# Batch 1's first dense layer by seven products instead of eight, in a newly planned order (sliding-window attention followed by a squared-ReLU layer, one Trainium2 core)

## The chip, the core and the metric

The kernel runs on one core of one Trainium2 chip. The metric is the device time of one execution in microseconds (us). The kernel before took 212.76 us (median of three runs, 212.1 to 213.73). The profile comes from one execution of its own; its span, from the first to the last instruction, is 210.2 us.

A core has five engines that run at the same time and wait for each other through semaphores: TensorE (PE in the profile, with PEld for its weight loads), VectorE (DVE), ScalarE (ACT), GpSimd (POOL) and SyncE (SP, which here only issues DMAs). TensorE writes to PSUM; VectorE and ScalarE fetch results from there.

## The reference

Four batches of 768 tokens, 8 heads of 64. Each query sees the last 128 keys and the first four ("sinks"). The heads side by side give x with 512 columns, and a dense layer, ReLU, square, dense layer follow:

```python
keep = is_sink | in_window            # 4 sinks, window 128
a = softmax(where(keep, q @ k.T / 8, -1e9))
x = (a @ v)                           # as 3072 tokens x 512
h = x @ w_in                          # 512 x 2048
r = np.maximum(h, 0.0)
g = r * r
return g @ w_out                      # 2048 x 512
```

## The kernel before, in words

A batch is three pairs of token tiles (s = 0, 1, 2, of 256 tokens each). For each pair the attention runs in groups: scores into PSUM (tile `ps`, line 607), the exponential by ScalarE (`expm`, line 628), the mask by VectorE (lines 637, 640) or by a GpSimd select (line 215), the product with the values (`po`, line 676), the normalisation by VectorE (lines 692, 693, into `xn_sb`). Then x is transposed: in batches 0 and 1 by TensorE (`px`, line 725) with a copy into `xT`, in batches 2 and 3 by DMA.

The first dense layer exists in two forms. `layer1` (line 757) is the plain one: 16 blocks of 128 features, four matmuls per block and 256 or 512 tokens; then a ReLU (lines 768, 770) and a square (lines 777, 779) of each PSUM tile. `layer1_fast` is a scheme of the kind of Strassen's: it halves features, inner dimension and tokens, forms sums of the x halves (`xs`, line 845; for one pair of tiles alone they are first spread into `xd`) and of the weights (`weight_sums_in`, `wi`, line 803, and sums written over `w_in_sb`, line 811), and needs seven half-size products instead of eight. The function `quad` makes one group of them: products 1, 2, 5, 4, 3, 6, 7 (line 887) into two PSUM regions, with work between them: a copy `t` of the first region (ScalarE or VectorE, line 189 or 191), two subtractions from it by VectorE (line 928), a ReLU (line 943), and at the end a combined add and ReLU by VectorE alone (line 955), and two squares (lines 909, 911). Product 5 waits for the copy, products 4 and 3 for the two subtractions, 6 and 7 for the ReLU.

Before, batches 2 and 3 use the fast form (pair 0 by itself, in products of 128 columns; pairs 1 and 2 together, in products of 256 columns), batches 0 and 1 the plain one. The second dense layer has the same two forms (`layer2`, line 976, for two thirds of batch 0; `layer2_fast`, line 1086, for all the rest).

All work is recorded as operations in a `Plan` and issued in the order that the string `ORDER` at the top of the file gives: one number for each operation, with a letter where the engine was chosen (d VectorE, a ScalarE, g GpSimd) and a `+n` where a pool of rooms was chosen. PSUM has two pools of two rooms each (`att`, `den`), and an operation may get a room from one or the other. So each engine's queue is fixed by hand ahead of time, in order, and an instruction that waits holds up all behind it on its engine.

`weight_sums_in` keeps two of the five rooms of the pool `qr`, in which the loads of q and k land too. `load_natural` issues the loads of batches 2 and 3 from GpSimd's queue; SyncE transposes q and k by DMA.

Of the kernel before, what the change touches and what calls it, by code (L numbers as in the profile page):

```python
# [21 lines left out]
0 7 8 9 1 5 10 11 2 12 13 3 14 15 55d 57+0 16 19 59a 20 17 56d 21 18 61d 63+0 22 58 62d 65a 60d 64 6 67a 83+1 79 66a  # L22
68d 69+1 85 70 71d 103+0 84+0 105 73g 74d 72d 23 75+1 86 76 77d 91+0 78a 24 87+1 93 25 89 88 92+0 80 26 114+1 90 94
95+0 4 96 117 97 106g 99+1 98 104+0 107 100d 101 118g 81+1 102d 113+0 108d 156 115 127 27 28 29 30 31 32 33 34 35 36
37 38 116d 82 109+0 111 39 40 41 119+1 121 157a 158a 110 112 120 122 162 123+1 125 163d 168 169d 126a 124a 171 172a
170a 159 160d 177 128 131 165 173d 161d 132d 178d 166d 164a 130a 129a 133a 144 146 136 138 174 145 137 289 290 148
134 175a 140 135 176a 147d 167d 139d 291 179d 292 293 141d 142 143 149g 42 43 44 45 46 150 151 47 48 49 50 51 52 53
54 365 366 367 368 208g 369 370 371 372 373 294 295 152 154 296 153d 155d 297d 298d 186 187d 180 181a 200+0 204+1
192+0 201 193 205 194a 206d 195a 189 207d 182d 203a 196+0 197 183 198a 190a 191a 188d 199d 202d 274 212+0+0 184d 209
278 279 215 213 237+0+0 210+1 211 238 240 185d 300 301 275 214 302 241d 276 277 303 280 281 282 304 219+0+0 283 222  # L30
220 306a 305 307 230+0+0 309a 233 231 308 311 223 216 221 310 239d 224+0 312 234g 232g 299 385 386 384 383 313 225
314 242+0 217+0 243 218 284 315 316 235+0 236 285 251+0 286a 287a 317d 252d 253d 244+0 246 226+1 228 247d 227d 245a
248+1 229a 399 322 249d 250d 402 400 323d 355 401 256+0+0 259 257 340 254+0 255 341a 258d 358 356 342a 396 260d 334
335a 374 375 376 377 378 379 380 381 395g 388 390 387 288 392 391 318 389 393 394 331 263+0+0 332a 261+1 264 266 319
262 267d 324d 406 333a 407 320a 337 409 265g 382 597 268+0 598 599 600 601 602 603 604 605 606 607 608 609 610 338a
321d 403 269 328 627d 410 270+0 272 404 408 329a 271a 273d 359 325 405 339a 336a 326a 346 347d 357 327a 415 418 419d
330d 352 411 353a 416 412 354d 447 448 343 344a 345a 349 422 423 425 417g 426g 611 451 452 397 363 449 453d 350d 398
450 351a 348a 454 455 457 466 456a 438 458 459 441 439 467 485 486 489 490 487 460 488 461 361 492 431 491a 432 434
615 413 616 622 620 619 493 462 494d 468 463 464a 414 465 621 617 618 420 440g 612 424g 427 496 433g 442g 428 498
421 470 471 443 435g 436 472a 504a 495 362 499 497 500 473 444 437 508 505 469 628 501 475d 474 477 647 429 625 445  # L40
430 446 650 502a 648 624 503 623 626 360 476 478 481 507 479 506 480 364 482 483d 523+0 525a 524 631 527 526 528 634
632 509+0 510 529 511d 512 530 531a 654 538 633 539 513 514 515 655 533 534 657 649g 656g 516 517a 638 613 614 535
635 536d 537 641 519 520 532a 636 658g 651g 521 639 569+0 570 637 571a 629 583+0 630 572 573 585a 640 522a 518a 574
584 587 575 576 586 555+1 642 589 577a 588 643 679 557a 540 556 590 559 591a 592a 578a 558 560 579 580 593 594 581
561 562 595 541+0 542 683 563a 564a 543d 545 544 680 546 565 547 566 548 684 686 644 567 685a 596a 549a 582a 681
550d 689 682 645 484 646 670 551 552 687 690 673 671 674g 553 688a 554a 663 691 694 666 664 665g 568d 698 692 693
699 659 652 702 703 705 667g 672g 695 696d 700 653 717 660 718 721 668 697 661 736a 704a 669 737 675 676 701 722 739
740 738 708 677 678 662 755+1 706 709 741+1 742 757a 719 720 756 743a 723a 707d 759 745 724 758 761 725 744 760 762
763a 764a 711 746 727 710 713 726a 765 766 747 712 769 714 771 767 728 730 715d 772 748 749a 729 815+0 816 817a 732
770 731 818 733 819 751 752 787+1 734a 735 716 801+0 802 803a 789a 753 820 804 768d 821 788 822 773+1 805 791 754a  # L50
823a 824a 775a 790 806 750d 792 829 807 774 793 776 825 808 794 826 809a 827 830 831 795a 796a 810a 777 779 811 778
812 797 798 833 780 834 836 813 799 828a 835a 781a 832 838d 839 783 784 782a 800a 814a 837 840 841 844 785 786d 842
848 849 852 853 855 843 845 846d 867 854a 850 851 858 857d 868 871 847 856 859 873a 861 862 860 863 864 869 872 865a
866 870 877 874 876a 875 878 880 881 886 879 882 883 885 884
# [59 lines left out]
def kernel(  # L114
# [267 lines left out]

    def load_natural(b, s, older_values):
# [36 lines left out]
    def attention(b, key):  # L420
# [3 lines left out]
        begun = [ops["layer1", b - 1, 0, 0]] if b >= 2 and b not in NATURAL else []  # L424
# [12 lines left out]
        def stage(g, f0, f1, side):  # L437
# [4 lines left out]
            def at(f):  # L442
                return key(f0 + (f1 - f0) * f)
# [94 lines left out]
            if g == 0:  # L538
                def sink_keys(e):
                    for h2 in range(2):  # L540
                        r = slice(64 * h2, 64 * h2 + 64)
                        nc.vector.tensor_copy(
                            out=kb[r, :].rearrange("p (m c) -> p m c", c=136)[:, :, 4 * h2:4 * h2 + NSINK],
                            in_=qkT_sb[r, :, 1, 0, 0:NSINK])
# [11 lines left out]
                A["sink_keys"] = op(at(0.1), {"dve": 0.34}, sink_keys,  # L556
# [189 lines left out]
    def layer1(b, key, fbs, c0, cw, need):  # L746
# [3 lines left out]
        bs, rs = Slot("den", 1), Slot("r", 1)  # L750
# [10 lines left out]
        ops["layer1", b, fbs[0], c0] = a  # L761

# [97 lines left out]
    def quad(b, ss, qd, key, xs, sums, slots, part, landed, whole):  # L860
# [15 lines left out]
        def product(name, bk, n, fresh, after):  # L876
# [19 lines left out]
            ops["layer1", b, (f0, name), ss[0]] = o  # L896
            return o
# [19 lines left out]
        m1 = product(1, 0, 0, True, [o for x, o in ops.items() if x[0] == "layer1" and x[1] == b - 1])  # L917
# [43 lines left out]
    def layer2(b, u, keys, by_part=False):  # L961
        P.group = ("l2", b, u)
        bs = Slot("den", 2)
# [57 lines left out]
    def layer2_fast(b, u, key):  # L1021
# [33 lines left out]
        bs, os_, us = Slot("den", 1 if tail else 2), Slot("osb", 1), Slot("u", 1)  # L1055
        ys = Slot("att", 1) if tail else bs
# [84 lines left out]
        pairs = out[128 * g:128 * g + 256, :].rearrange("(i p) m -> p i m" if b in FAST and u else "(p i) m -> p i m", i=2)  # L1141
# [23 lines left out]
        def store_rest(e):  # L1165
            o = bank_t["osb", b, u]
            if b not in FAST or not u:
# [15 lines left out]
    NATURAL, TURNED, BIASED, FAST = (2, 3), (), 1, (2, 3)  # L1183
# [24 lines left out]
    for b in range(B):  # L1208
        if b == 0:
# [3 lines left out]
            at(1, 0.2, 0.725, "att")  # L1213
# [4 lines left out]
        elif b in FAST:  # L1218
            layer1_fast(b, (0,), lambda i, b=b: b + 0.167 * i / 2, 0.01)
            layer1_fast(b, (1, 2), lambda i, b=b: b + 0.167 + 0.34 * i / 4, 0.01)  # L1220
        else:
            for i, fb in enumerate(range(0, NFB, 2)):
                layer1(b, b + 0.34 * i / 8, (fb, fb + 1), 0, 512, (0, 1))
        for i, fb in enumerate(range(0, NFB, 4) if b not in FAST else ()):
            if b == 0:
                layer1(b, 0.2 + 0.226 * i / 4, range(fb, fb + 4), 512, 256, (2,))
            else:
                layer1(b, b + 0.34 + 0.167 * i / 4, range(fb, fb + 4), 512, 256, (2,))
        if b + 1 == FAST[0]:
            weight_sums_in(b + 0.4, [ops[x] for x in ops if x[0] == "layer1" and x[1] == b])  # L1230
        if b + 1 < B:
# [7 lines left out]
            else:  # L1239
                attention(b + 1, lambda f, b=b: b + LO + (HI - LO) * f)(0, 0.0, 1.0, "att")  # L1240
        if b == 0:
            weight_sums(0.6, [w_out_op[i] for i in range(4)])
        for u in range(NS):
            if b == 0 and u < 2:
# [40 lines left out]
```

## Time and profile before

| | before |
|---|---|
| time of the runs | 212.76 us (212.1, 213.73) |
| profiled execution: span | 210.2 us, granted TensorE clock 0.997 |
| TensorE busy | 201.4 us (96%), 2383 matmuls |
| weight loads (PEld) | 169.4 us (81%) |
| VectorE busy | 170.8 us (81%) |
| ScalarE busy | 126.6 us (60%) |
| GpSimd busy | 101.8 us (48%) |
| DMA | 26.09 MB, mean 124 GB/s |

The profiled execution's own time is its span of 210.2 us and what lies around it; the median of the runs is 2.56 us above that span. A matmul's row lasts about 0.16 us longer than the distance to the next one, because matmuls are pipelined; prices of matmuls are therefore read from the length of runs of them in the chain of waits. On VectorE and ScalarE too, rows that follow each other overlap by about 0.07 us.

### The profile page before, as it was taken

Reading aid. Unit: us, or ns where it says so; the run is one execution under the profiler, and the core shown is the slowest. Engines: PE = TensorE matmul, PEld = TensorE weight load, DVE = VectorE, ACT = ScalarE, POOL = GpSimd, SP = SyncE. Lnnn points to the kernel's source line nnn. Section 1 sums busy time; section 2 is a strip of 40 time slices with the busy share of each in tenths; the row PEclk is TensorE's granted clock in tenths of the full one; section 3 lists DMA queues with packets and bytes.
Section 4 is the critical chain, followed back from the end, with each engine's and each line's share of the span. In section 5 each row is a group of like instructions: output and inputs, shape, how many; then the busy total and the mean of one; then the engine's idle time right before and its main releaser. Section 6 shows DMA issues by size and latency. Waiting matters only on the chain.

```text
span 210.2 us, 5719 instructions
## 1 busy us (share of the span) xinstructions
PE 201.4 (96%) x2383; PEld 169.4 (81%) x2383; DVE 170.8 (81%) x317; ACT 126.6 (60%) x162; POOL 101.8 (48%) x143
## 2 busy tenths in 40 slices
PE   3999999999999999999999999799999999999993
PEld 3859996689468845679789988699899999999892
DVE  7487567366999964789997988999989978999863
ACT  2498287407744579898952268889870244896110
POOL 7999774898877941999369023700253000000000
PEclk9999999999999999999999999999999999999998
DMA  5999999999999999999987639700512300400222
GB/s 171 278 188 206 171 201 214 161 155 205 153 112 157 104 150 252 138 124 144 149 102 151 103 77 179 50 3 0 150 62 69 75 5 38 166 0 0 103 100 100
DMA packets 93881, 26.09 MB, mean 124 GB/s; under 512 B 86816, under 2 KB 91552, under 8 KB 93856
## 3 DMA queue, kind: packets, MB, share of 16 engines
q0 software_dynamic: 69248, 12.59, 81.3%
q1 hardware_dynamic: 24424, 13.07, 27.9%
q8 instruction: 18, 0.29, 0.6%
q10 hardware_dynamic: 184, 0.07, 0.1%
q14 instruction: 7, 0.06, 0.1%
HBM read 27.30 MB, written 6.29 MB: 160 GB/s over the span
## 4 chain that ended last, share of the span: by engine, by line
PE 94%; DVE 2%; ACT 1%; POOL 1%; issue 1%; POOLq 0%; DVEq 0%
PE py L1086 29%; PE pm L757 20%; PE pm L887 17%; PE po L676 7%; PE py L976 7%; PE ps L607 6%; PE pt L500 3%; PE pt L182 2%; PE px L725 1%; ACT expm L628 1%; PE ya L1086 1%; PE ps L600 1%; PE pk L566 1%; DVE r L955 1%; DVE gT_sb L911 0%
## 5 line engine op out<-in xcount | busy, mean ns | idle before, releaser
L215 POOL TENSOR_SCALAR_AFFINE_SELECT expm<-expm 128x512 bf16<-128x512 bf16 x42 | 29.2, 724 | 49.5 <-ACT expm L628 24.5
L628 ACT ACTIVATE expm<-ps 128x1024 bf16<-128x1024 f32 (+1 forms) x48 | 43.8, 950 | 12.4 <-PE ps L607 11.3
L757 PE MATMUL pm<-xT,w_in_sb 128*128 128x256 bf16 (+1 forms) x320 | 44.7, 294 | 0.0
L757 PEld LDWEIGHTS <-w_in_sb 128*128 128x128 bf16 x320 | 34.2, 114 | 6.6 <-issue 0.9
L1086 PEld LDWEIGHTS <-gT_sb 128*128 128x128 bf16 x336 | 31.1, 98 | 4.2 <-issue 0.5
L1086 PEld LDWEIGHTS <-sg 128*128 128x128 bf16 x240 | 22.8, 98 | 3.3 <-issue 0.5
L768 ACT ACTIVATE r<-pm 128x1024 bf16<-128x1024 f32 x14 | 14.3, 1022 | 13.5 <-PE pm L757 13.4
L887 PEld LDWEIGHTS <-w_in_sb 128*128 128x128 bf16 x256 | 21.8, 114 | 0.5 <-issue 0.2
L887 PE MATMUL pm<-xs,wi 128*128 128x128 bf16 (+1 forms) x192 | 19.5, 246 | 1.5 <-DVE xs L845 0.9
L1086 PE MATMUL py<-wt,gT_sb 128*128 128x256 bf16 x160 | 20.8, 273 | 0.0
L1086 PE MATMUL py<-wt,sg 128*128 128x256 bf16 x160 | 20.6, 273 | 0.0
L909 ACT ACTIVATE gT_sb<-r 128x1024 bf16<-128x1024 bf16 x18 | 18.4, 1051 | 0.3
L1086 PE MATMUL py<-w_out_sb,gT_sb 128*128 128x256 bf16 x144 | 18.5, 273 | 0.0
L189 ACT ACTIVATE osb<-py 128x256 f32<-128x256 f32 (+1 forms) x15 | 6.2, 410 | 20.3 <-DMA out_dram<-osb 6.0
L770 DVE TENSOR_SCALAR r<-pm 128x1024 bf16<-128x1024 f32 x10 | 12.2, 1222 | 7.5 <-PE pm L757 4.3
L887 PEld LDWEIGHTS <-wi 128*128 128x128 bf16 x192 | 16.4, 113 | 2.2 <-issue 2.1
L693 DVE TENSOR_TENSOR xn_sb<-po,rc 128x512 bf16<-128x512 f32 (+1 forms) x28 | 17.2, 615 | 1.0
L676 PEld LDWEIGHTS <-expm 128*128 128x128 bf16 x352 | 16.3, 97 | 1.4 <-issue 0.5
L676 PE MATMUL po<-v,expm 128*128 128x65 bf16 x352 | 17.3, 193 | 0.1
L943 ACT ACTIVATE r<-pm 128x1024 bf16<-128x1024 f32 x12 | 12.1, 1021 | 8.1 <-PE pm L887 7.9
L928 DVE TENSOR_TENSOR t<-t,pm 128x512 f32<-128x512 f32 x24 | 15.9, 680 | 0.9 <-ACT t L189 0.4
L955 DVE CUSTOM_DVE_ANT_1 r<-pm,t 128x1024 bf16<-128x1024 f32 x12 | 14.5, 1220 | 1.6 <-PE pm L887 1.5
(97 smaller groups left out, 381.9 us busy)
## 6 DMA issues: line engine op xcount, KB each, us to landing
out_dram<-osb SPq DMA_DIRECT2D x11, 512.0 KB, 4.5
v<-in_v_dram POOLq DMA_DIRECT2D x24, 128.0 KB, 7.1
qn<-in_k_dram POOLq DMA_DIRECT2D x20, 128.0 KB, 7.1
qn<-in_q_dram POOLq DMA_DIRECT2D x20, 128.0 KB, 6.9
w_in_sb<-in_moe_w_in_dram POOLq DMA_DIRECT2D x4, 512.0 KB, 10.2
w_out_sb<-in_moe_w_out_dram POOLq DMA_DIRECT2D x4, 512.0 KB, 10.4
qr<-in_k_dram SPq DMA_DIRECT2D x4, 256.0 KB, 5.1
qr<-in_q_dram SPq DMA_DIRECT2D x4, 256.0 KB, 4.8
```

What stands on the lines that cost most here:

```text
L215: nc.gpsimd.affine_select(out=e_tile, in_=e_tile, compare_op=ALU.is_ge, fill=fill, base=i - 1, pattern=[[0, n], [1 if i else -1, 128]], ch ...
L628: nc.scalar.activation(out=x[:, :, o:512], in_=bank_t["s", b, s, m][:, :, o:512], func=AF.Exp, scale=scale)
L676: touch(("po", b, s, m0), e, nc.tensor.matmul(pv[:, i, h2, :], lhsT=lhsT, rhs=rhs, start=(n_ == 0), stop=(n_ == len(mms) - 1)), j)
L693: touch(("po", b, s, m0), e, nc.vector.tensor_tensor(out=xn_sb[:, 2 * s:2 * s + 2, 128 * (m0 + j0):128 * (m0 + j0 + nj)].rearrange("p i (j ...
L757: nc.tensor.matmul(pm[:, i, :], lhsT=w_in_sb[:, fb // 4, kb, fb % 4:512:4], rhs=xT[:, c0 // 256:(c0 + cw) // 256, kb, :], start=(kb == 0), ...
L768: nc.scalar.activation(out=o, in_=h, func=AF.Relu)
L887: touch(tag, e, nc.tensor.matmul(y[:, bk, i, :], lhsT=weights(name, f0 + i, a), rhs=rhs[:, a, :], start=fresh and i == 0 and a == 0, stop= ...
L909: nc.scalar.activation(out=d, in_=x, func=AF.Square)
L928: touch(tag, e, nc.vector.tensor_tensor(out=T["t"], in0=T["t"], in1=T["y"][:, bk], op=ALU.subtract), bk)
L955: touch(tag, e, nc.vector._custom_dve(TENSOR_ADD_SAT, out=r.rearrange("p b n c -> p b (n c)"), in0=T["y"].rearrange("p b n c -> p b (n c)" ...
L976: touch((b, u), e, nc.tensor.matmul(pm[:, i, :], lhsT=gT_sb[:, fb, 128 * t:128 * t + 128], rhs=w_out_sb[:, fb, :], start=(fb == 0), stop=( ...
L1086: ins = nc.tensor.matmul(y_, lhsT=x[:, i, :], rhs=r_, start=(first or tail and n == 2) and i == 0, stop=i == HB - 1, skip_group_check=not ...
```

## The change

`FAST` becomes a table of which pairs of tiles of which batch use `layer1_fast`. Batch 1 enters it: pairs 0 and 1 together (four groups of products of 256 columns) and pair 2 by itself (two groups of 128 columns). The weight sums are then formed before batch 1's first dense layer instead of after it. Several operations get the choice between both PSUM pools. The copy of the sink keys may go to ScalarE or VectorE. Where two pairs of tiles were done together, the output rows are stored in their natural order. The string `ORDER` and with it each engine's queue is new from the eleventh entry on; it was made by a replay that counts shared SBUF ports and PSUM reads.

```diff
-0 7 8 9 1 5 10 11 2 12 13 3 14 15 55d 57+0 16 19 59a 20 17 56d 21 18 61d 63+0 22 58 62d 65a 60d 64 6 67a 83+1 79 66a
...
+0 7 8 9 1 5 10 11 2 12 3 55d 13 57+0 14 56d 15 19 20 16 21 61d 59a 17 22 63+0 18 6 62d 58 79 65a 64 60d 67a 68d 83+1
...
-        begun = [ops["layer1", b - 2, 0, 0], w_out_op[3]]
+        begun = [first_layer1[b - 2], w_out_op[3]]
...
-                if b - 1 in FAST:
+                if b == 3:
                     o.after += [ops["wi", 1, 0]]
...
-                        nc.vector.tensor_copy(
-                            out=kb[r, :].rearrange("p (m c) -> p m c", c=136)[:, :, 4 * h2:4 * h2 + NSINK],
-                            in_=qkT_sb[r, :, 1, 0, 0:NSINK])
+                        copy(e, kb[r, :].rearrange("p (m c) -> p m c", c=136)[:, :, 4 * h2:4 * h2 + NSINK],
+                             qkT_sb[r, :, 1, 0, 0:NSINK])
...
-                A["sink_keys"] = op(at(0.1), {"dve": 0.34}, sink_keys,
+                A["sink_keys"] = op(at(0.1), {"dve": 0.34, "act": 0.42}, sink_keys,
...
-        bs, rs = Slot("den", 1), Slot("r", 1)
+        bs, rs = Slot(("den", "att"), 1), Slot("r", 1)
...
-        bs, os_, us = Slot("den", 1 if tail else 2), Slot("osb", 1), Slot("u", 1)
-        ys = Slot("att", 1) if tail else bs
+        bs, os_, us = Slot(("den", "att"), 1 if tail else 2), Slot("osb", 1), Slot("u", 1)
+        ys = Slot(("att", "den"), 1) if tail else bs
...
-        pairs = out[128 * g:128 * g + 256, :].rearrange("(i p) m -> p i m" if b in FAST and u else "(p i) m -> p i m", i=2)
+        natural = any(u in ss and len(ss) == 2 for ss in FAST.get(b, ()))
+        pairs = out[128 * g:128 * g + 256, :].rearrange("(i p) m -> p i m" if natural else "(p i) m -> p i m", i=2)
...
-    NATURAL, TURNED, BIASED, FAST = (2, 3), (), 1, (2, 3)
+    NATURAL, TURNED, BIASED = (2, 3), (), 1
+    FAST = {1: ((0, 1), (2,)), 2: ((0,), (1, 2)), 3: ((0,), (1, 2))}
+    CLASSIC2 = ((0, 0), (0, 1))
...
+        if done and 1 not in {x[1] for x in ops if x[0] == "wi"}:
+            weight_sums_in(b + 0.4, [o for x, o in ops.items() if x[0] == "layer1"])
+        for ss in done:
+            if b == 1:
+                layer1_fast(b, ss, (lambda i: 1 + 0.34 * i / 4) if ss == (0, 1) else (lambda i: 1.34 + 0.167 * i / 2), 0.01)
+            elif ss == (0,):
+                layer1_fast(b, ss, lambda i, b=b: b + 0.167 * i / 2, 0.01)
             else:
-                layer1(b, b + 0.34 + 0.167 * i / 4, range(fb, fb + 4), 512, 256, (2,))
-        if b + 1 == FAST[0]:
-            weight_sums_in(b + 0.4, [ops[x] for x in ops if x[0] == "layer1" and x[1] == b])
+                layer1_fast(b, ss, lambda i, b=b: b + 0.167 + 0.34 * i / 4, 0.01)
```

More of the change, by code (lines that the diff above doesn't have):

```diff
@@ L423, in attention @@
         groups = GROUPS[b]
-        begun = [ops["layer1", b - 1, 0, 0]] if b >= 2 and b not in NATURAL else []
+        begun = []
         prev_tr = [ops[x] for x in ops if x[0] == "transpose" and x[1] == b - 1]
@@ L915, in square @@
                 ops["sq", b, f_, c_, w_, r] = o
-        m1 = product(1, 0, 0, True, [o for x, o in ops.items() if x[0] == "layer1" and x[1] == b - 1])
+        m1 = product(1, 0, 0, True, [])
         m2 = product(2, 1, 1, True, [])
@@ L1217 @@
                     layer1(b, 0.083 * i + 0.042 * s, range(4 * i, 4 * i + 4), 256 * s, 256, (s,))
[L1218 to L1221, printed above, removed]
+        elif (0, 1) not in done and b == 1:
             for i, fb in enumerate(range(0, NFB, 2)):
                 layer1(b, b + 0.34 * i / 8, (fb, fb + 1), 0, 512, (0, 1))
-        for i, fb in enumerate(range(0, NFB, 4) if b not in FAST else ()):
-            if b == 0:
-                layer1(b, 0.2 + 0.226 * i / 4, range(fb, fb + 4), 512, 256, (2,))
-            else:
-                layer1(b, b + 0.34 + 0.167 * i / 4, range(fb, fb + 4), 512, 256, (2,))
-        if b + 1 == FAST[0]:
-            weight_sums_in(b + 0.4, [ops[x] for x in ops if x[0] == "layer1" and x[1] == b])
+        if b < 2 and (2,) not in done:
+            for i, fb in enumerate(range(0, NFB, 4)):
+                if b == 0:
+                    layer1(b, 0.2 + 0.226 * i / 4, range(fb, fb + 4), 512, 256, (2,))
+                else:
+                    layer1(b, b + 0.34 + 0.167 * i / 4, range(fb, fb + 4), 512, 256, (2,))
+        if done and 1 not in {x[1] for x in ops if x[0] == "wi"}:
[5 more added lines that the diff above has]
+                layer1_fast(b, ss, lambda i, b=b: b + 0.167 * i / 2, 0.01)
+            else:
+                layer1_fast(b, ss, lambda i, b=b: b + 0.167 + 0.34 * i / 4, 0.01)
         if b + 1 < B:
```

81 lines of the change are left out of this document (44 added, 37 removed).

## The prediction

> **What bounds the kernel now.** I read the page first: which engine is full, in which slices, and which chain ended last.
>
> ```profile
> span 210.2 us, 5719 instructions
> ...
> PE 201.4 (96%) x2383; PEld 169.4 (81%) x2383; DVE 170.8 (81%) x317; ACT 126.6 (60%) x162; POOL 101.8 (48%) x143
> ...
> PE 94%; DVE 2%; ACT 1%; POOL 1%; issue 1%; POOLq 0%; DVEq 0%
> ```
>
> TensorE is busy 96% of the span and is 94% of the chain. What shortens TensorE's list shortens the kernel, unless VectorE (81%) or ScalarE falls behind at some place. So next the chain in order of time (start, length, what), for prices and for gaps.
>
> ```profile
> 22.49 6.99 PE pm L757 x64
> ...
> 73.14 1.85 PE pm L757 x8
> ...
> 123.90 0.89 PE pm L887 x16
> ...
> 128.13 1.92 PE pm L887 x32
> ...
> 130.18 1.22 DVE r L955
> 131.41 0.61 DVE expm L637
> 132.02 1.04 DVE gT_sb L911
> 133.06 0.78 DVE xs L845
> ```
>
> 64 matmuls of 256 columns in 6.99 us are 109.2 ns each; 16 of 128 columns in 0.89 us are 55.7 ns; eight of 512 columns take 1.85 us behind a group of scores and 1.75 otherwise, so a restart behind scores costs 0.1. Batch 1's plain first layer runs from 73.14. The only stretch away from the start in which the chain leaves TensorE for long is 130.2 to 133.9, in batch 2's first layer, the fast form: TensorE waits there for VectorE's queue. Third, the windows of batch 1's and batch 2's first layer (length, then busy time of PE, PEld, DVE, ACT, POOL).
>
> ```profile
> 73.00:100.00 27.00, 27.00 (x272) 18.26 (x268) 20.16 (x38) 24.13 (x27) 19.14 (x25) 1.00 2.15 161
> ...
> 124.00:151.00 27.00, 25.46 (x321) 23.33 (x319) 25.90 (x41) 23.52 (x29) 7.41 (x11) 1.00 0.44 74
> ```
>
> In batch 1 TensorE never idles and VectorE has 7 us to spare; in batch 2 VectorE is full and TensorE isn't. The change gives batch 1 the work of batch 2.
>
> Fourth, prices on VectorE and ScalarE, from the groups by form (mean ns of one behind the busy time).
>
> ```profile
> L928 DVE TENSOR_TENSOR t<-t,pm 128x512 f32<-128x512 f32 x24 | 15.9, 680 | 0.9 <-ACT t L189 0.4
> L955 DVE CUSTOM_DVE_ANT_1 r<-pm,t 128x1024 bf16<-128x1024 f32 x12 | 14.5, 1220 | 1.6 <-PE pm L887 1.5
> L943 ACT ACTIVATE r<-pm 128x1024 bf16<-128x1024 f32 x12 | 12.1, 1021 | 8.1 <-PE pm L887 7.9
> L909 ACT ACTIVATE gT_sb<-r 128x1024 bf16<-128x1024 bf16 x18 | 18.4, 1051 | 0.3
> ```
>
> **The change, part by part.** *Products.* Removed: 64 matmuls of 256 columns and 64 of 512. The nine pieces of them in the chain between 73.14 and 99.60 add up to 21.43 us. Added: four groups of seven products of four matmuls, 112 of 256 columns (12.23 us), and two groups of seven products of eight, 112 of 128 columns (6.24), with five restarts behind scores or sinks (0.5): 18.97. Nothing else in TensorE's list changes in number. Gain 2.45 us, all of it on the path.
>
> A rule speaks against the narrow half of that. The Trainium skill (TensorE: Matmul & The Clock Gate, Back-to-back issue gap) says that in a stream of weight loads and matmuls one of 128 columns takes about 81 ns, and that 56 ns holds for the isolated gap. By that the 112 would cost 9.07 us as an estimate, and the sum below would end at 214.5 instead of 211.7. The trace doesn't agree: 16 of them, each with its own weights, in 0.89 us.
>
> *VectorE and ScalarE.* Six groups add 12 subtractions (8.2 us at 0.68), six first copies (3.6 at 0.60, all on ScalarE) and the x sums (3.4). The 12 ReLUs become six plain and six combined ones of the same length, but a combined one can only be VectorE's. Four small products of the sink values (0.28 each) go from VectorE to GpSimd. Over the whole run VectorE gets about 11 us more, ScalarE about 6: they still fit. Not in the stage itself: batch 1's new first layer gives TensorE 22.2 us up to the first product of batch 1's second layer, and the orders put about 22.5 us of VectorE's work and 23 of ScalarE's beside it, because four exponentials of batch 2 stand there too.
>
> How much that stalls I count on the one chain that is longest in the new orders. It starts where TensorE ends the last two transposes of batch 1's first 512 tokens. ScalarE's copy of them: 0.60. VectorE: four `xs`, two masks, one `osb`, six subtractions from `t` (0.68 each), a ReLU (1.22), two combined ReLUs (1.22 each), a reciprocal with its normalisation (0.89); by the rows 12.9 us in 18 instructions, 11.7 with an overlap of 0.07 between neighbours. ScalarE: three squares, one copy, the spreading `xd` (1.05), four exponentials of 0.81, two copies `t`, two ReLUs; 11.3 us in 13, 10.5 with the overlap. VectorE again: two subtractions and a combined ReLU, 2.4, which frees the PSUM room of the next product. Hand-overs 0.4, and four instructions that wait for the one just before them on their own engine, 0.1 each: 26.0 us. TensorE's list over the same stretch: 112 matmuls at 109.2 ns (12.2), 96 at 55.7 (5.3), 48 value products at 30 (1.5), six groups of scores (3.0), other products and transposes (1.5), five restarts (0.5): 24.0. So TensorE stands still for 2.0 us at least.
>
> The same count for batch 2 in the kernel before gives 1.3. The trace lost more: from 123.90 to 161.96 TensorE's list is 112 at 55.7, 208 at 109.2, 120 value products at 30, 2.9 of scores and 0.5 of restarts, together 35.9 of 38.06 us, a loss of 2.1. I add that difference of 0.8 and take 2.8 us for the new stall. From below 1.3, if the copies run earlier than I string them; from above 5, if collisions (below) hit often.
>
> *Batch 2's stall.* In the new order the copies and sums of batch 2 stand further ahead of TensorE's need. The same count leaves 0.7 of 2.1, a gain of 1.4; bounds 0 and 2.1.
>
> *Weight sums.* Ten additions (0.68 to 0.79) move from batches 1 and 2 into the first 73 us, of which 6 before batch 0's first layer ends. VectorE was busy 17.6 of the 28 us from 17 to 45 and hides them. Without that cover they would cost 7 us.
>
> *Queues.* On GpSimd four products of sink values (0.49 each) now stand ahead of the fourth load of `w_out`, which landed at 39.8 and was needed at 42.2: 0, at most 0.6. Batch 2's loads start some 10 us later, because two rooms of `qr` are taken by the weight sums; SyncE's transposes (5.3 us to landing) follow later too, but batch 2's first scores come some 14 us later in TensorE's list. One copy of sink keys (two instructions, 0.2 each on VectorE, not above the 0.28 of ScalarE's smallest row) goes to ScalarE and waits there for a transposed load of batch 3; a square and two exponentials are queued behind it, and TensorE's value products wait for those. The load (7.1 to landing) and the transpose (5.3) leave about 1 us of margin plus the new stall. I take 0 for all queues and keep 1.5 above.
>
> *Sum.* −2.45 + 2.8 − 1.4 = −1.05. The span of 210.2 becomes 209.15; with the 2.56 us between this span and the median of the runs, 211.7.
>
> **The rivals.**
>
> *The new stall doesn't come.* If VectorE's and ScalarE's queues meet TensorE better than my chain, the products' 2.45 and up to 1.8 of the old stall are both gained: 208.5. For it: batch 0 and the stretch from 161.96 to the tail keep TensorE without a gap at VectorE shares of 88%. Against it: the stage asks as much of VectorE as of TensorE.
>
> *VectorE becomes the bound, through collisions with GpSimd.* The timeline shows one:
>
> ```profile
> 97.48 0.68 DVE L779 TENSOR_TENSOR gT_sb<-r 128x1024 bf16<-128x1024 bf16 x1
> 98.08 1.13 DVE L1044 TENSOR_TENSOR sg<-gT_sb 128x1024 bf16<-128x1024 bf16 x1
> 99.24 1.01 DVE L1044 TENSOR_TENSOR gT_sb<-gT_sb 128x1024 bf16<-128x1024 bf16 x1
> ...
> 98.00 1.70 POOL L215 TENSOR_SCALAR_AFFINE_SELECT expm<-expm 128x512 bf16<-128x512 bf16 x2
> ```
>
> Beside two selects, two VectorE instructions with both inputs in SBUF take 0.33 and 0.45 us more. Batch 2's stage had 7.4 us of GpSimd's work beside it; batch 1's has 16 selects between its first layer and the middle of its second. If ten of them hit an instruction on the path at 0.39, that is 3.9 us: 215.6. It decides from about eight on, when the kernel is slower than before by over 1%. Against it: rows that read PSUM keep their length (the 24 subtractions lie within 673 and 689 ns), and GpSimd's DMA issues slow nobody. The Trainium skill (SBUF — State Buffer, Who interferes with whom) states an exclusive lock, the loser waiting for the whole instruction; by that ten hits would cost about 6 us, 217.7 as an estimate, and the rows show less.
>
> *The stall eats all*: 5 us in batch 1 but 2.1 saved in batch 2, 213.1.
>
> *Narrow products paced by their weight loads* (the page's rule, as a mechanism here): at the 114 ns of a weight load's row the 112 would cost 6.5 more, 218.2. Batch 2's own narrow products run at 55.7.
>
> **How the numbers follow.** Forecast 0.45, no new stall 0.27, collisions 0.19, all eaten 0.08, narrow products 0.01. About 1% (2.1 us) is what a measurement tells from no change. Faster by over 1%, below 210.6: the second case and a small part of the first, 0.33. Slower by over 1%, above 214.9: 0.18. Within: 0.49. The range, 208.2 to 215.2, takes in the case without a stall and most of the collisions; the forecast's own is 210.2 to 213.2.
>
> **What would show it.** Right: `L887` with some 112 more matmuls of each width at the same distances, 18.5 us; in batch 1's stage VectorE at 95% or more, TensorE with waits on VectorE's or ScalarE's `r`, `t` or `xs` of about 3 us together; batch 2's stage with TensorE waits under 1 us; no wait on a load. Wrong: TensorE without a gap in batch 1 (the chain count failed), gaps behind rows of 1.0 us and more that were 0.7 (collisions), or a wait on `w_out_sb` or on a transposed load.

## The result, and the profile after

| | before | changed |
|---|---|---|
| median of the runs | 212.72 us (211.99 to 213.73, 18 runs) | 214.18 us (213.04 to 216.06, 18 runs) |
| changed / before | | 1.0068, 95% interval 1.0045 to 1.0092 |
| profiled execution: span | 210.2 us | 211.5 us |
| second profile of each (from the experiments): span | 210.9 us | 212.3 us |

The kernel became 0.7% slower; 0.5% faster was forecast. Ratios here leave out runs in which the chip was disturbed, medians hold all runs, so the two can differ a little.

The page of the changed kernel, the same lines as before:

```profile
span 211.5 us, 5938 instructions
...
PE 199.7 (94%) x2474; PEld 173.5 (82%) x2479; DVE 182.3 (86%) x331; ACT 131.9 (62%) x173; POOL 104.1 (49%) x143
...
PE 83%; DVE 7%; DMA 3%; issue 2%; SPq 2%; ACT 1%; DVEq 0%; ACTq 0%
```

TensorE's busy time did get shorter, by 1.7 us here (five matmul rows that this trace lacks are a part of that) and by 0.6 between the second profiles. But TensorE is no longer alone on the chain: VectorE has 7% of it instead of 2%, and SyncE's queue (SPq) appears. Where TensorE stands still, the waits of the changed kernel say (engine and line, what it waited for: us in total, times, the longest):

```profile
PE py L1092 <- DVE gT_sb L1050: 1.2, 1, 1.2
PE pm L892 <- DVE t L934: 0.7, 1, 0.7
...
PE ps L611 <- DVE r L961: 0.7, 1, 0.7
PE py L1092 <- DVE osb L1117: 0.3, 1, 0.3
```

Only the second of these stands in batch 1's new first layer (at 88 us). The other three stand behind it, at 104 to 111 us, in batch 1's second layer and the scores beside it, where the prediction had no stall. The windows of these two stretches and of batch 2's first layer (length, busy time of PE, PEld, DVE, ACT, POOL):

```profile
74.00:98.00 24.00, 23.23 (x320) 20.97 (x318) 23.30 (x38) 22.66 (x30) 14.00 (x21) 1.00 1.64 164
98.00:118.00 20.00, 17.84 (x235) 15.08 (x232) 19.19 (x33) 12.01 (x18) 17.45 (x21) 1.00 2.15 163
129.00:145.00 16.00, 16.00 (x211) 15.34 (x211) 15.58 (x28) 14.32 (x18) 1.63 (x3) 1.00 0.39 93
```

In the kernel before, batch 1's second layer looked like this (its second profile):

```profile
100.00:118.00 18.00, 18.00 (x255) 15.19 (x254) 16.69 (x30) 11.30 (x15) 10.58 (x15) 1.00 1.27 130
```

In the second window of the changed kernel VectorE is at 96% and GpSimd at 87%, and TensorE stands still for 2.2 us; before, they were at 93% and 59%, and TensorE did not stand still. In batch 2's first layer, where the kernel before lost its 2 us, TensorE here has no gap.

For all comparisons below, TensorE's *loss* in a stretch is the distance between the starts of its rows in the timeline, less their number times the usual distance of their width in the same traces (218.5, 109.2, 55.7 ns for 512, 256, 128 columns, 30.3 for value products, 54.7 and 45.7 for scores). It holds restarts of 0.1 to 0.2 as well as waits. The end is the time from the start of TensorE's last group to the end of the span.

| us | 74-98 | 98-118 | 118-129 | 129-145 | end |
|---|---|---|---|---|---|
| before, two profiles | 0.4, 0.4 | 0.3, 0.3 | 0.4, 0.4 | 2.1, 2.1 | 4.6, 4.6 |
| changed, two profiles | 2.1, 1.9 | 2.9, 2.8 | 0.3, 0.3 | 0.4, 1.3 | 5.2, 5.2 |

From the second profile of before to that of the changed kernel: +1.5, +2.5, -0.1, -0.8, +0.6, and +0.3 in all other places: 4.0 us more lost. The span is 1.4 longer, so the list itself is 2.6 us shorter; by the row prices it should be 2.5 (64 matmuls of 256 and 64 of 512 columns removed, 20.97; 112 of 256 and 112 of 128 added, 18.47). The start of the first layer's first product (16.8 and 17.5 us in the profiles of before, 17.4 and 17.4 in the changed ones) is chance: it lies between 16.9 and 18.3 in the experiments, whose queues are the same up to there. The expectation below counts it from the scores just ahead, some 0.4 earlier.

### The profile page after: what moved, and what is told of

Same layout as the page of the kernel before. It is cut to its first block, busy times and chain, and to the rows that moved or that the text cites. A ratio compares the mean times of both kernels' runs of the same rounds, so it can differ in the third digit from the quotient of the medians.

```text
span 211.5 us, 5938 instructions
## 1 busy us (share of the span) xinstructions
PE 199.7 (94%) x2474; PEld 173.5 (82%) x2479; DVE 182.3 (86%) x331; ACT 131.9 (62%) x173; POOL 104.1 (49%) x143
## 4 chain that ended last, share of the span: by engine, by line
PE 83%; DVE 7%; DMA 3%; issue 2%; SPq 2%; ACT 1%; DVEq 0%; ACTq 0%
PE py L1092 28%; PE pm L892 23%; PE pm L761 10%; PE py L982 6%; PE po L680 6%; PE ps L611 5%; DMA qr<-in_q_dram 3%; PE pt L505 2%; DVE r L961 2%; DVE t L934 2%; SPq L349 2%; PE px L729 1%; DVE gT_sb L1050 1%; PE ya L1092 1%; DVE xn_sb L697 1%
## 5 line engine op out<-in xcount | busy, mean ns | idle before, releaser
L892 PEld LDWEIGHTS <-w_in_sb 128*128 128x128 bf16 x384 | 32.6, 114 | 2.2 <-issue 1.7
L915 ACT ACTIVATE gT_sb<-r 128x1024 bf16<-128x1024 bf16 x29 | 30.1, 1056 | 2.4 <-DVE r L961 2.1
L892 PE MATMUL pm<-xs,wi 128*128 128x256 bf16 (+1 forms) x288 | 29.2, 246 | 0.0
L934 DVE TENSOR_TENSOR t<-t,pm 128x512 f32<-128x512 f32 x36 | 23.6, 680 | 0.9 <-ACT t L192 0.2
L892 PEld LDWEIGHTS <-wi 128*128 128x128 bf16 x288 | 23.9, 114 | 0.4 <-issue 0.3
L961 DVE CUSTOM_DVE_ANT_1 r<-pm,t 128x1024 bf16<-128x1024 f32 x18 | 21.6, 1217 | 1.0 <-PE pm L892 0.7
L761 PE MATMUL pm<-xT,w_in_sb 128*128 128x256 bf16 x192 | 22.2, 273 | 0.0
L761 PEld LDWEIGHTS <-w_in_sb 128*128 128x128 bf16 x192 | 20.6, 114 | 0.7 <-issue 0.5
L892 PE MATMUL pm<-xs,w_in_sb 128*128 128x256 bf16 (+1 forms) x192 | 19.8, 246 | 0.8 <-DVE t L934 0.7
L949 ACT ACTIVATE r<-pm 128x1024 bf16<-128x1024 f32 x17 | 17.1, 1019 | 3.7 <-PE pm L892 3.5
L611 PE MATMUL ps<-qkT 64*128 64x128 bf16 (+1 forms) x256 | 14.6, 238 | 0.7 <-DVE r L961 0.7
```

What stands on the lines that cost most here:

```text
L611: nc.tensor.matmul(ps[:, h2, o:o + w], lhsT=qkT_sb[r, m, 1, c, :], rhs=qkT_sb[r, m, 0, qb:qb + w // 128, :], start=(i == 0 and not biased) ...
L761: nc.tensor.matmul(pm[:, i, :], lhsT=w_in_sb[:, fb // 4, kb, fb % 4:512:4], rhs=xT[:, c0 // 256:(c0 + cw) // 256, kb, :], start=(kb == 0), ...
L892: touch(tag, e, nc.tensor.matmul(y[:, bk, i, :], lhsT=weights(name, f0 + i, a), rhs=rhs[:, a, :], start=fresh and i == 0 and a == 0, stop= ...
L915: nc.scalar.activation(out=d, in_=x, func=AF.Square)
L934: touch(tag, e, nc.vector.tensor_tensor(out=T["t"], in0=T["t"], in1=T["y"][:, bk], op=ALU.subtract), bk)
L949: touch(tag, e, nc.scalar.activation(out=r, in_=T["y"], func=AF.Relu), 0, 1)
```

## The experiments

**Second profiles of both kernels** (no edit).

> The kernel before, unchanged, for a second profile. In nine profiles of the new order TensorE's first product of the first layer starts at 17.0 to 18.0 us, in the one profile of the kernel before at 16.4; each engine's queue up to there is the same in both. Theory (the first loads land at another time in each execution): here it starts anywhere between 16.4 and 18.0, so the 0.6 us of start in the ledger is chance. Rival (the change costs it): 16.4 again. In the middle TensorE's only loss over 0.5 us is the one at 130 to 134 us.

Measured: span 210.9, first product at 17.5 instead of 16.8 (by the expectation's count 17.1 instead of 16.4): the start is chance. The loss at 129 to 145 us is 2.1 as in the first profile. Between 85 and 140 us the waits show only one instruction that waits for a DMA, a copy on ScalarE into `osb`, 3.0 us for an output store.

> The changed kernel, unchanged, for a second profile on the chip of the two kernels beside it. Theory (batch 2's and batch 3's loads come about 5 to 10 us later than before, and what waits for a transposed load differs from run to run): wait of ScalarE's sink keys' copy 0 to 2.4 us and/or of VectorE's sums for the transposed x 0 to 2.4 us; span 211 to 214. Rival (the waits in the other profiles came from their edits): the same profile as the first, 0.4 and 0.

Measured: 213.86 us (213.21 to 215.27), ratio 1.0062 (1.0033 to 1.0090). The copy of the sink keys waits 1.3 us for its transposed load (0.4 in the first profile), VectorE's sums 1.1 us for the transposed x (0 in the first). So what waits for a transpose differs between executions of the same kernel, and the first profile's quiet batch 2 was luck: nine profiles keep this part of the order and leave nothing out (these two, tail_order, vector_order, keys_later, masks_vector, subtract_first and the two four_orders below), and two of them lose under 0.5 us at 129 to 145 us, the other seven 1.3 to 2.7.

**The order of the last stores.**

```diff
-929 934 931+0 932 935 933a 936 939 937 938 940 941 943 942
+929 934 931+0 932 935 933a 936 939 937 938 943 940 942 941
```

> The changed kernel with only the order of SyncE's last three entries as in the kernel before: the two stores of finished rows of the last pair are issued ahead of the operation that holds the last quarter's store. Theory (the store queue at the end costs 0.65 us): the time from TensorE's last product to the end of the span falls from 4.1 us to 3.5, and the median falls by about 0.65 us against the changed kernel's 214.18 (to some 213.5). Rival (the last store's landing decides, in whatever order they are issued): no change of the median, and the distance from the last product to the end stays 4.1.

SyncE's queue at the end of the changed kernel, and of this one:

```profile
207.39 0.34 SPq L1163 DMA_DIRECT2D out_dram<-osb  x1
207.79 0.42 SPq L1182 DMA_DIRECT2D out_dram<-osb  x1
208.26 0.92 SPq L1179 DMA_DIRECT2D out_dram<-osb  x2
```

```profile
209.52 0.34 SPq L1182 DMA_DIRECT2D out_dram<-osb  x1
210.13 0.82 SPq L1179 DMA_DIRECT2D out_dram<-osb  x2
211.05 0.40 SPq L1163 DMA_DIRECT2D out_dram<-osb  x1
```

In the changed kernel the store that waits for TensorE's last product stands in front of three that are ready, and each takes 0.3 to 0.5 us of SyncE; turned round, they leave while TensorE still works. Measured: the end is 4.6 us, as before, instead of 5.2; it is 4.5 to 4.6 in all six kernels below that have this order and 5.1 to 5.3 in all others. Median 213.69, ratio 1.0027 (0.9998 to 1.0055). The 0.6 us are shown by the profiles; in the times of the runs they are less sure, since this interval still touches that of the changed kernel (1.0045 to 1.0092).

**Is it VectorE's load, its order, or collisions?** Three kernels: two entries of VectorE's queue moved (a mask behind, a sum ahead); GpSimd's masks of batch 2 left out; three of VectorE's masks left out.

```diff
-... 506 507 467 461+0 ... 513d 514 465 517 542 518 524 543 516
+... 506 507 461+0 ... 513d 514 467 465 517 542 543 518 524 516
```

> The changed kernel with two operations of VectorE's queue moved: a mask of batch 2 goes behind a combined ReLU and two evictions of batch 1's second layer, and the second weight-side sum of pair 2 goes ahead of an output addition and of a sum for pair 1. Nothing is left out. Theory (TensorE waits 2.2 us between 104 and 111 us only because VectorE works off its queue in the wrong order): these three waits (0.66, 0.27, 1.24) shrink to 0.3 together and the span falls by about 1.9. Rival (VectorE is simply full from 80 to 112 us and the load decides): the waits move to other products behind, and the span falls by less than 0.7.

Measured: median 216.84, ratio 1.0155 (1.0088 to 1.0222). The loss at 98 to 118 us is 2.6 instead of 2.9. The theory failed, and the rival fits better: this turn of the order alone gives nothing.

```diff
+                            if (b, s) == (1, 2) and e == "dve" or (b, s, m) == (2, 0, 1):
+                                return
```

> The changed kernel without three masks on VectorE beside batch 1's first layer (two of batch 1's pair 2, one of batch 2's pair 0; 1.9 us of VectorE; those keys stay unmasked). Theory (VectorE is the bound from 80 to 112 us): the wait of 0.7 us at 88 goes, and the waits between 104 and 111 shrink too, because the queue is 1.9 us ahead: span -1.5 to -1.9. Rival (only the second layer's own queue counts): -0.7 at most, the waits at 104 to 111 stay. Rival (the first layer's stall is ScalarE's): no change at 88.

Measured: median 215.53, ratio 1.0075 (1.0038 to 1.0113). The wait at 88 us is 0.76 by the starts of TensorE's rows, as in the changed kernel, although 1.4 us of the masks left out stood ahead of it (the third stands behind). So that wait is not VectorE's load. And the loss at 98 to 118 us is 6.7, not less. This profile is of an execution of 217.4 us, 1.9 above the kernel's median. ScalarE's timeline in it shows where the loss begins (start, length, line, operation; in brackets the idle time before and what ended it):

```profile
105.82 0.44 ACT L192 ACTIVATE kblk<-qkT 64x16 bf16<-64x16 bf16 x2 [2.40 <-DMA qkT<-qn]
106.28 1.06 ACT L917 ACTIVATE gT_sb<-r 128x1024 bf16<-128x1024 bf16 x1
```

The copy of batch 3's sink keys waited 2.4 us for a transposed load, and the last square of batch 1 was queued behind it; VectorE's sums for TensorE's next product came after that. There they met selects: an addition took 2.37 us instead of 0.42, and the two sums 2.56 instead of 1.29.

```diff
-                            elif e == "dve":
+                            elif e == "pool" and b == 2:
+                                pass
+                            elif e == "dve":
```

> The changed kernel without GpSimd's masks of batch 2 (14 selects; those keys stay unmasked). Theory (collisions with GpSimd's selects are what makes VectorE late in batch 1's second layer): VectorE's instructions with both inputs in SBUF between 98 and 111 us go from 1.0 to 1.1 us back to 0.68 (masks to 0.55), some 2.5 us of VectorE's time, TensorE's waits of 0.66, 0.27 and 1.24 us go to less than 0.3 together, span about -2.0. Rival (load and order of the queue): rows become shorter but the waits stay above 1.5 us, span -0.5 or less. Rival (the DMA issues of GpSimd, not the selects, slow the two rows at 98.6 and 99.5): these two stay at 1.0 and 1.1.

Measured: ratio 1.0072 (1.0037 to 1.0106). VectorE's rows go back to 0.68 and 0.55, but here too the copy waited 2.15 us, so TensorE still lost 2.1 at 98 to 118 us. That leaves it undecided; the two causes had to be taken away together.

**The copy further back, alone and without the selects.**

```diff
-... 454+0 495+0+1 685a 421a 496 ... 455 521a 477+0
+... 454+0 495+0+1 421a 496 ... 455 521a 685a 477+0
```

> The changed kernel with ScalarE's copy of batch 3's sink keys moved six ScalarE instructions further back in its queue (behind the first quarter of batch 1's output). Theory (this copy waits 0 to 2.4 us for a transposed load that comes at another time in each execution, and a square and two exponentials of ScalarE, then VectorE's sum, then TensorE's product wait behind it): the wait of ScalarE for a transposed load between 101 and 108 us is gone; TensorE's loss between 104 and 116 us, 2.4 to 5.8 us in the profiles so far, is 2.0 or less; the median falls by 0.5 to 1.5 us from 214.18 and the spread of the runs gets narrower. Rival (VectorE's load and collisions make that loss, the copy's wait is covered): the loss stays at 2.2 or more and the median within 0.3.

Measured: ratio 1.0091 (1.0067 to 1.0116), loss 2.9 unchanged: the rival was right. A wait of 0.4 is covered by VectorE's lateness, and so is the 1.3 of the second profile (loss 2.8); the copy cost TensorE where it waited over 2 us (less_vector, no_selects).

> keys_later, and without GpSimd's masks of batch 2 (14 selects; those keys stay unmasked). Theory (the loss between 104 and 116 us has two parts, the copy's wait and VectorE's collisions with the selects): with both gone TensorE loses less than 0.7 us there. Rival (VectorE is full by its own load): still 1.5 or more.

Measured: the loss at 98 to 118 us is 0.2 (before: 0.3). This is the verdict on the second layer: collisions, with the copy as a second cause where it is late. The timeline of VectorE and of GpSimd's selects at this place, first in the changed kernel:

```profile
98.57 0.99 DVE L641 TENSOR_TENSOR expm<-expm,mask 128x768 bf16<-128x768 bf16 x1
99.48 1.11 DVE L1050 TENSOR_TENSOR sg<-gT_sb 128x1024 bf16<-128x1024 bf16 x1
...
101.23 1.05 DVE L1050 TENSOR_TENSOR sg<-gT_sb,sg 128x1024 bf16<-128x1024 bf16 x1
...
108.19 2.15 DVE L1050 TENSOR_TENSOR gT_sb<-gT_sb 128x1024 bf16<-128x1024 bf16 x2
...
101.05 1.73 POOL L218 TENSOR_SCALAR_AFFINE_SELECT expm<-expm 128x512 bf16<-128x512 bf16 x2
...
106.23 3.57 POOL L218 TENSOR_SCALAR_AFFINE_SELECT expm<-expm 128x512 bf16<-128x512 bf16 x4
```

then without the selects:

```profile
98.91 0.55 DVE L641 TENSOR_TENSOR expm<-expm,mask 128x768 bf16<-128x768 bf16 x1
99.38 0.68 DVE L1052 TENSOR_TENSOR sg<-gT_sb 128x1024 bf16<-128x1024 bf16 x1
...
100.70 0.69 DVE L1052 TENSOR_TENSOR sg<-gT_sb,sg 128x1024 bf16<-128x1024 bf16 x1
...
106.17 1.29 DVE L1052 TENSOR_TENSOR gT_sb<-gT_sb 128x1024 bf16<-128x1024 bf16 x2
```

The same two sums end at 110.3 in one kernel and at 107.5 in the other. Nine rows from 98.5 us on are longer with the selects, by 0.1 to 0.44 each and 3.2 us together. The time is then lost elsewhere: at 118 to 129 us TensorE loses 3.5, because ScalarE waits 5.0 us for an output store and 4.0 us for the transposed x, and TensorE itself 1.1 us for transposed q and k. The ratio stays at 1.0077 (1.0052 to 1.0101).

**The same masks on VectorE** (four of them, 2.7 us of work; nothing left out).

```diff
-... 659 474g 660 ... 663 476g 664 ... 524 543 516 ... 481g 483g
+... 659 660 ... 663 664 ... 524 543 474d 476d 516 ... 481d 483d
```

> The changed kernel with four masks of batch 2 on VectorE instead of GpSimd, the first two of them behind the sums of batch 1's second layer. Nothing is left out; VectorE gets four instructions of 0.68 more, GpSimd loses eight selects. Theory (the 2.3 us that TensorE loses between 104 and 111 us are collisions with those selects, not VectorE's load): the loss there falls to 0.7 or less although VectorE has 2.7 us more to do, VectorE's two sums ahead of TensorE's product take 1.3 instead of 2.15, and the median falls by 1.0 to 2.0 us against the changed kernel's 213.9 to 214.2. Rival (VectorE's load): the loss grows to 4 or more and the median rises.

Measured: ratio 1.0133 (1.0092 to 1.0174), loss 3.6. Neither forecast: the two sums take 1.72 instead of 2.15, not 1.3, because four of GpSimd's remaining selects now stand beside them, from 107.3 us; the two new masks behind the sums take 2.15 beside the same selects. The copy waited 1.7 us here, and TensorE then waited 1.0 for a normalisation that stands behind these masks. In the combination with the copy moved (below) the loss is 2.0, and 0.7 with two masks more on VectorE. So VectorE can carry these masks, but not in any order.

**The stall in the first layer.** In VectorE's queue the subtraction for product 4 goes ahead of the combined ReLU of the group before.

```diff
-... 389a 373 376 379 456+0+0 378 381
+... 389a 376 379 456+0+0 378 373 381
```

> The changed kernel with one pair of VectorE's queue turned round at 87 us: the subtraction that product 4 of the last group of pairs 0 and 1 waits for goes ahead of the combined ReLU of the group before. Theory (the wait of 0.7 us at 88 us is the order inside a group, 1.2 us of ReLU in front of what TensorE needs next, and not VectorE's load; it stayed at 0.76 when three masks of VectorE were taken away): the wait is gone (0.1 or less), and what was lost there is lost again later in part, because VectorE's queue decides from 94 us on: median -0.2 to -0.7. Rival (VectorE's load): the wait moves to the next product and stays at 0.7.

Measured: ratio 1.0095 (1.0063 to 1.0128). Product 4 no longer waits, but TensorE waits 0.87 us one product later, for sums of x that now stand behind the ReLU. The wait did not shrink, it moved: in either order one thing that TensorE needs next stands behind 1.22 us of ReLU. No run here takes this wait away.

**SyncE's queue.** It issues the transposes of q, k (`qkT`) and x (`xT`). The changed kernel, 111 to 131 us (start, length, x number):

```profile
111.21 1.19 SPq L711 DMA_TRANSPOSE xT<-xn_sb  x1
112.50 0.53 SPq L1170 DMA_DIRECT2D out_dram<-osb  x1
113.13 4.01 SPq L459 DMA_TRANSPOSE qkT<-qn  x3
117.20 3.19 SPq L711 DMA_TRANSPOSE xT<-xn_sb  x2
...
127.81 2.56 SPq L711 DMA_TRANSPOSE xT<-xn_sb  x2
```

A transpose takes mostly 1.2 to 1.3 us of the queue (2.0 at most here), and from 113.1 to 130.4 twelve of them follow each other with at most 0.1 us between them. In the kernel before the last transposes of batch 2's x were issued by 124.8 us, here by 130.4 (before):

```profile
121.00 3.84 SPq L707 DMA_TRANSPOSE xT<-xn_sb  x3
```

 The loads come later too: batch 2's first at 61.1 us instead of 50.4, batch 3's first at 90.8 instead of 85.5, after GpSimd had waited 4.4 us for a transpose to free the room.

```diff
-... 502 680 683 711+0+0 ... 487 503 560
+... 502 711+0+0 ... 487 503 680 683 560
```

> The changed kernel with two transposes of batch 3's q and k moved on SyncE's queue behind the last two transposes of batch 2's x. Theory (batch 2's x of pairs 1 and 2 is sometimes late because those two transposes, 3.4 to 3.9 us of SyncE's queue, stand ahead of it): the wait of VectorE's sums for the transposed x at 132 to 134 us (2.4 us in two of four profiles of this order) is gone and TensorE's loss there of 1.9 us too; in the median some -0.5 to -1.0 us. Rival (what is late is the row of transposes before, so that the two last ones only follow): the wait stays, median within 0.3.

Measured: ratio 1.0130 (1.0091 to 1.0169). VectorE's wait for x is gone, and TensorE instead waits 2.4 us for a transposed q.

> The changed kernel with all three orders together: the stores at the end as in tail_order, the sink keys' copy as in keys_later, the x transposes as in x_first. Nothing is left out. If the parts add up (-0.65, -0.5 to -1.5, -0.5 to -1.0) the median is 211.2 to 212.5 and the kernel is as fast as the one before (212.7) or up to 0.7% faster. If the waits only move on, it stays above 213.2.

Measured: ratio 1.0113 (1.0052 to 1.0174); TensorE waits 0.9 for the same q.

> The changed kernel with batch 3's loads of q and k ahead of its loads of v in GpSimd's queue, and three of SyncE's transposes of batch 3 ahead of the first transpose of batch 2's x (in the gap of 5 us that SyncE has there). Nothing is left out. Theory (late transposed loads cost 0 to 2.6 us): no wait of ScalarE, VectorE or TensorE for a transposed q, k or x; TensorE's loss from 129 to 145 us 0.4 or less; median 0.5 to 1.0 below that of the changed kernel in the same call and half its spread; the loss of 2.2 us at 104 to 111 us stays, being the collisions'. Rival (SyncE's queue as a whole is full, any order has something late): a wait for another transposed tile of 1 us or more.

> loads_turns with the order of the last stores as in the kernel before. Theory (parts add): 0.65 below loads_turns, some 212.6, within 0.3% of the kernel before. Rival: the store order is worth nothing, equal to loads_turns.

Measured: ratios 1.0183 (1.0152 to 1.0215) and 1.0115 (1.0092 to 1.0139). In the profile of the first, VectorE's sums waited 4.2 us for the transposed x at 137 us: the rival held. GpSimd's queue now ran its selects in one row, and in the profile of the second, an execution 3.4 us above that kernel's median, this cost more than anything else (timeline, VectorE and GpSimd):

```profile
108.96 4.91 DVE L1050 TENSOR_TENSOR gT_sb<-gT_sb 128x1024 bf16<-128x1024 bf16 x2
110.29 4.08 POOL L218 TENSOR_SCALAR_AFFINE_SELECT expm<-expm 128x512 bf16<-128x512 bf16 x6
```

Two sums that take 1.29 alone take 4.91; TensorE waits 4.2 for them and loses 7.8 at 98 to 118 us. In the profile of the first the same two took 2.1; they ended 0.4 us after the row of selects began.

**The four turns together.** four_orders is masks_vector, subtract_first, keys_later and tail_order; four_orders_b has two masks more on VectorE; the five_orders kernels add three transposes of batch 3 ahead of x.

> The changed kernel with masks_vector, subtract_first, keys_later and tail_order together. Nothing is left out. If the shown parts add up: against a profile of the changed kernel (212.3) -0.65 for the stores, -1.6 to -2.3 for the collisions, -0.3 to -0.7 for the subtraction: span 208.7 to 209.8, median 210.6 to 211.7, which is 0.5 to 1.0% below the kernel before. If late transposed loads take it back: 212.5 to 213.5.

> four_orders with two masks more of batch 2 (pair 2) on VectorE. If collisions with those selects at 108 to 113 us still cost TensorE something, it is faster than four_orders by up to 0.5 us; if VectorE's load decides by then, slower by up to 1.4.

Measured: ratios 0.9996 (0.9970 to 1.0021) and 0.9997 (0.9977 to 1.0016): the 0.7% are won back, and nothing above; had the parts added up, four_orders would be 0.5 to 1.0% below the kernel before. The end is 4.6 again, and in four_orders_b, which leaves nothing out, the loss at 98 to 118 us is 0.7 although VectorE does six of the masks itself. What remains is 2.3 in the first layer and 2.1 at 118 to 129 us, the latter by the waits:

```profile
ACT osb L192 <- DMA out_dram<-osb: 4.1, 1, 4.1
ACT xd L192 <- DMA xT<-xn_sb: 2.9, 1, 2.9
```

> four_orders_b with three of SyncE's transposes of batch 3 (678, 677, 679) moved ahead of the first transpose of batch 2's x, into SyncE's gap at 106 to 110 us. Nothing is left out. Theory (what is left in four_orders_b, 1.8 us of TensorE at 124 to 127, is ScalarE waiting 2.9 us for the second half of that x, whose transpose is issued at 116.2 behind those three): the transpose is issued at about 111.5, ScalarE's wait is under 0.5, TensorE's loss at 118 to 129 us falls from 2.1 to 0.5, and the median of 213.0 falls by 0.7 to 1.6 us, below the kernel before (212.8). Rival (the lateness only moves to the x of pairs 1 and 2): the wait for x at 133 us is 1 us or more and the median stays within 0.5.

> five_orders without the turned pair of subtract_first (the combined ReLU goes ahead of the subtraction again). Theory (turning them moved TensorE's wait from product 4 to the sums of x one product later, 0.76 against 0.87 us): the same median as five_orders within 0.3 us. Rival: slower by 0.5 or more.

Measured: ratios 1.0161 (1.0121 to 1.0201) and 1.0131 (1.0111 to 1.0151). The two differ by 0.2 us in the median, as forecast for the turned pair. In five_orders ScalarE's wait for x went, as intended, but an output store was now late:

```profile
ACT osb L192 <- DMA out_dram<-osb: 8.1, 1, 8.1
...
PE py L1092 <- ACT osb L192: 2.8, 1, 2.8
```

In five_orders_c VectorE's sums waited 2.6 us for the transposed x of pairs 1 and 2. The rival was right in its kind: what went ahead in this queue made another thing late. No version measured beats the kernel before.

## Why the prediction was wrong, by its steps

*Products: right.* -2.45 forecast with restarts; the ledger leaves -2.6 without, against -2.5 by the row prices. The new narrow products follow each other at 56 ns, as in batch 2; pacing by weight loads did not occur. The Trainium skill's 81 ns (TensorE: Matmul & The Clock Gate, Back-to-back issue gap) does not hold in this trace either.

*New stall in the first layer: mis-sized and for the wrong reason.* 2.8 forecast; 1.5 more lost at 74 to 98 us. Half of that is one wait, 0.76 us at 88; the rest is restarts and waits of 0.25 at most, which the forecast had set off against the restarts of the removed pieces. The chain count took VectorE's load as the cause; with 1.4 us of that load taken away ahead of it the wait was the same (less_vector). What stands ahead of it in VectorE's queue is a combined ReLU of 1.22 and the subtraction, with 0.44 us of scores as TensorE's only cover. The count also had all six first copies on ScalarE: one, of 0.68 us, is VectorE's, at 85.9 us, just ahead of this wait.

*Second layer: the step that failed.* The count ended at its first product and put 0 behind it. There 2.5 us were lost. VectorE arrives with its queue full (96% from 98 to 118 us), and GpSimd's selects for batch 2, which the new order puts there, lengthen nine of its instructions by 3.2 us. That is the rival "collisions" in mechanism and place, and nearly in price: it took 0.39 for each hit, an instruction on the path that is lengthened, and the nine cost 0.36 on average. The mistake was to hold the hits out of the sum and give them a chance of 0.19, although by the prediction's own count about eight of them decide. Without the selects, and with the copy moved, the loss is 0.2 (keys_no_selects); with most of them on VectorE, and nothing left out, it is 0.7 (four_orders_b). Single hits do not show the worst price: one sum of 0.68 took 3.88 beside six selects in a row in loads_turns_tail. On this the trace now agrees with the Trainium skill (SBUF — State Buffer, Who interferes with whom: a VectorE instruction with two inputs in SBUF contends with a GpSimd instruction that reads SBUF, and the ports that they share are an exclusive lock): in masks_vector a sum and two masks of 0.68 take 1.11 to 1.12 by turns with selects of 0.62 that take 1.08 to 1.12.

*Batch 2's stall: right in kind, but the size differs between executions.* -1.4 forecast; -1.7 in the first profile, -0.8 in the second, +0.5 in tail_order's. VectorE's old queue there is gone as forecast, but in most profiles the wait for the transposed x stands in its place.

*Queues at 0: wrong.* The stores at the end cost 0.6 us (tail_order). The copy on ScalarE was named with a margin of about 1 us; it waited 0 to 2.4, and cost TensorE when it was over 2. "Batch 2's loads start some 10 us later" was right (10.7), but the text looked only at the scores behind them; SyncE's transposes of x for batch 2 and of batch 3 were pushed together, and this queue has nothing to spare there. That the two rooms of `qr` cause the lateness is argued from the order of rooms, and not tried.

Taken together, from the second profiles: -2.6 + 1.5 + 2.5 - 0.1 - 0.8 + 0.6 + 0.3 = +1.4, against -1.05 forecast. The median, 214.18, lies inside the range, on its other side.

## What to carry to other kernels

Count a chain of waits beyond the stage that is changed, until the fuller engine has slack again: a queue that arrives full pays for everything that the next stage does to it. When a change moves loads, follow every transfer behind them through the queue that issues it, to its last user, since in a queue without gaps what goes ahead makes something else late. When a rival's price and number of hits are known, put the product into the sum. And take a second profile before pricing a wait for a DMA: two executions of one kernel put it at different places.

## What the runs showed of the hardware

- A transpose by DMA held SyncE's queue for 1.19 us at least, mostly 1.2 to 1.3 and 2.4 at most (36 of them in the changed kernel); the twelve from 113.1 to 130.4 us fill it for 17 us.
- Two VectorE sums of 128x1024 with both inputs in SBUF: 1.29 us alone, 2.15 beside four selects that take turns with them, 2.56 in less_vector, 4.91 in the one execution in which one of them stood over six selects in a row. An addition of 128x256 in f32: 0.42 alone, 0.85 beside them, once 2.37.
- GpSimd's DMA issues alone lengthen none of these rows: without the selects all stay at 0.68 and 0.55 beside them (keys_no_selects). In the kernels with selects some long rows stand beside what the profile shows as DMA issues, two in the changed kernel (0.99, 1.11) and two in loads_turns (0.85, 1.11). GpSimd's rows are placed roughly in the profile, and whether a select stands there in truth stays open.
- Between the two executions of the changed kernel, the time from issue to landing of the same DMA differs by 1 us or more for 17 of the 103 DMAs whose landing the traces show, and by 2.4 at most.
